# One written order for the opening of a local-attention and mixture block

## The chip, the cores and the metric

The kernel runs on 1 core of one Trainium2 chip. The metric is the device time of one execution in microseconds. The engines are TensorE (PE, with its weight loads PEld), VectorE (DVE), ScalarE (ACT), GpSimd (POOL) and SyncE (SP), which issues the loads.

## What is computed

Attention over 4 batches, 8 heads, 576 positions and 64 columns, with a window of 128 and a bias that falls with distance; a gated layer on its result; then four small attention experts with a choice of two per position. The change is in the first two parts, whose reference is, cut:

```python
scores = np.where(mask, scale * (q @ kT) + bias, -1e9)       # mask: 0 <= i-j < 128
attn = softmax(scores);  x = attn @ v                        # -> [4, 576, 512]
h = np.maximum(x @ w_in, 0.0);  u, v = h[..., :512], h[..., 512:]
v_n = (v - mu) / np.sqrt(var + 1e-06)                        # over the last axis
v_s = np.einsum('ts,bsd->btd', w_spatial, v_n) + b_spatial[None, :, None]
gated = u * v_s                                              # then w_out and the experts
```

w_in (512 x 1024) comes as 64-bit floats. All matmuls that need precision are done as three passes over a high and a low part of each factor (PASSES, L36).

## The kernel before

**Decoding w_in.** Eight chunks of 128 x 512 numbers (512 KB each) are loaded (load_in, L191) and turned into a high and a low part. For chunk n, word_bits (L276) makes an absolute value on ACT (L281) and five operations on DVE (L284 to L289): max, shift, or, mask, multiply. add_in (L212) sums the two results on PE into a PSUM tile psw (two instructions with ident, one with one), and ACT copies the high part out. low_in (L225) makes the low part: for chunks 0 to 3 PE sums the same again into a second PSUM tile psl and subtracts the high part there (L231 to L233), and ACT copies it; for chunks 4 to 7 DVE subtracts (lo_part, L129). Chunks 0 to 3 hold the columns of v, 4 to 7 those of u.

**Attention.** Twenty tiles (b, j) of 128 positions, the fifth of a batch of 64. scores (L343) makes two halves g in PSUM (pool psS, two buffers); softmax (L361) runs per half on DVE a masked copy (L374, not for j = 0), four fused bias-and-minimum operations (L150), and at the end a sum, a reciprocal and a multiply (L380 to L382), with four exponentials on ACT between (L151). transposes (L385) turns the half on PE, ACT copies it (L393) and POOL cuts it in two by the window (L400, L401). attend (L404) multiplies with v, and take (L420) splits the result into x high (ACT) and x low (DVE, L129).

**Dense work of a batch.** v_tile (L431) five times with statistics, normalised (L457), u_half twice (L493, 96 matmuls together), spatial (L507, 112 matmuls, gate multiply at L523). It sits in the list Dense (L39) and is pulled by a credit, RATE = 8200 ns of planned cost a step, when its tile is ready; a list entry that is not ready takes the credit to 0.

**Order.** PE's instructions run in the order of the program; all other engines are ordered by the planner's own costs. The program of the opening: some steps by hand for tiles 0 and 1 (L570 to L602), then the loop over s (L606): step s attends tile s-2, makes the scores of tile s, turns tile s-1, runs the softmax of tile s, and pulls dense work between; parts(s) (L561) puts in the chunks 4 to 7 and, at s = 6 to 8, the spatial weights (setup, L247). A barrier without waits for the planner stands at the top of each step. At s = 9 the buffers of the opening are closed. Where s = 8 starts, 22 of the 112 spatial matmuls of batch 0 are done.

Of the kernel before, what the change touches and what calls it, by code (L numbers as in the profile page):

```python
# [9 lines left out]
F32 = mybir.dt.float32  # L10
# [3 lines left out]
U32 = mybir.dt.uint32  # L14
# [21 lines left out]
PASSES = ((0, 0), (0, 1), (1, 0))  # L36

# [65 lines left out]
def block_kernel(ctx, tc, qP, kP, v, w_in, wspT, bsp, w_outT, wcat, wo, rel, relt, low, tri, out):  # L103
# [97 lines left out]
    def bits(n):  # L201

        if not is64:
            return
        f = early.tile([P, 512], F32, tag="f", name=f"f{n}", bufs=2)
        w = u[n % 4][:, :512]
        live[n] += [w, f]

        for _ in word_bits(w, f, live[n][0], in_parts(n)[1]):
            pass  # L210

    def add_in(n):  # L212

        hi, lo = in_parts(n)
        if is64:
            w = live[n][1]
            ps = psD.tile([P, 512], F32, tag="D", name=f"psw{n}")
            nc.tensor.matmul(ps, ident, w, start=True, stop=False)
            nc.tensor.matmul(ps, one, lo, start=False, stop=True)
            live[n].append(ps)  # L220
            nc.scalar.copy(hi, ps)
        else:
            nc.scalar.copy(hi, live[n][0])

    def low_in(n):  # L225
        hi, lo = in_parts(n)
        if is64:
            w, ps = live[n][1], live[n][3]
            if n < 4:
                ps = psD.tile([P, 512], F32, tag="D", name=f"psl{n}")  # L230
                nc.tensor.matmul(ps, ident, w, start=True, stop=False)  # L231
                nc.tensor.matmul(ps, one, lo, start=False, stop=False)
                nc.tensor.matmul(ps, minus, hi, start=False, stop=True)  # L233
                nc.scalar.copy(lo, ps)
            else:
                lo_part(lo, ps, hi)
        else:
            lo_part(lo, live[n][0], hi)
        decoded[0] = n + 1
# [7 lines left out]
    def setup():  # L247
        def spatial_weights(k):
            s0, sn = TOK[k]
            st = d2.tile([P, S], F32, tag="f64w", name=f"st_wsp{k}", bufs=2)  # L250
            for r in range(0, P, sn):
                nc.sync.dma_start(st[r : r + sn, :], wspT[s0 : s0 + sn, :])
            yield
            nc.scalar.copy(wsp[0][:, k, :], st)
            yield
            lo_part(wsp[1][:sn, k, :], st[:sn, :], wsp[0][:sn, k, :])
            yield

# [65 lines left out]
    def load_chunk(b, j):  # L324

        q0, qn = TOK[j]
        Q_[b, j] = a1.tile([P, 4, P], F32, tag="q", name=f"q{b}_{j}", bufs=3)
        nc.sync.dma_start(Q_[b, j], qP[b, :, j])
        if j == 0:
            K_[b] = a1.tile([P, 4, S], F32, tag="k", name=f"k{b}")  # L330
        if b == 0:
            nc.sync.dma_start(K_[b][:, :, q0 : q0 + qn], kP[b, :, :, q0 : q0 + qn])
        elif j == 0:
            nc.sync.dma_start(K_[b], kP[b])
        V_[b, j] = a1.tile([P, 512], F32, tag="v", name=f"v{b}_{j}", bufs=5)
# [7 lines left out]
    def scores(b, j):  # L343
# [17 lines left out]
    def softmax(b, j, g):  # L361

        ps = st_[b, j, g]
        p = a1.tile([P, 4, P], F32, tag="p", name=f"p{b}_{j}_{g}", bufs=3)
        st = a1.tile([P, 8], F32, tag="stat", name=f"st{b}_{j}_{g}", bufs=4)
        if j == 4:
            nc.vector.copy_predicated(ps[:, :, 0:64], lowm[:, 128:192].unsqueeze(1).to_broadcast([P, 2, 64]), ps[:, :, 128:192])
            for h in range(2):
                row_softmax(p[:, h, :], ps[:, h, 0:P], reltail[:, 2 * g + h, :], st[:, h : h + 1], st[:, 4 + h : 5 + h])
            n = 2  # L370
        else:
            view = ps.rearrange("p o (h c) -> p (o h) c", h=2)
# [691 lines left out]
```

## Time and profile before

| | us |
|---|---|
| median of 3 runs (506.79 to 507.25) | 506.8 |
| the profiled execution | 506.48 |
| its span, first to last instruction | 504.7 |
| PE busy, weight loads busy | 483.2, 423.5 |
| DVE, ACT, POOL busy | 308.5, 260.7, 100.6 |
| mean granted PE clock | 0.993 of full |

Busy times are over the whole span. The opening, up to step s = 8 at 99.36 us, is a fifth of it. A matmul's busy time is modelled and overlaps the next one, so the cost of a matmul in a stream is the distance from one start to the next. A wait is named by what ended it. The kernel after ends its opening at the same step, s = 8.

### The profile page before, as it was taken

The page shows a single profiled execution, that of the slowest core. Times are in us where ns is not written, and L with a number is a line of the kernel's source. Part 1 is how long each engine was busy: PE and PEld are TensorE (multiplying, and loading weights), DVE is VectorE, ACT ScalarE, POOL GpSimd, SP SyncE. Part 2 cuts the span into 40 slices and gives each one's busy share as a digit, 9 for nine tenths or more (in the row PEclk, how much of TensorE's full clock was granted, in tenths as well). Part 3 has the DMA queues.
Part 4 walks back from the last instruction along what each step waited for, and adds up shares of the span by engine and source line. Part 5 has one row for each costly group of instructions (what it writes and reads, how often), then busy time and mean ns, then how long its engine had stood idle before and what let it go on. Part 6 is the DMA issues. An engine that isn't in the chain of part 4 may idle for free.

```text
span 504.7 us, 10536 instructions
## 1 busy us (share of the span) xinstructions
PE 483.2 (96%) x3910; PEld 423.5 (84%) x3910; DVE 308.5 (61%) x1069; ACT 260.7 (52%) x778; POOL 100.6 (20%) x209
## 2 busy tenths in 40 slices
PE   8979879999999999999999999999999999999995
PEld 6547668898988989899888999998888899897873
DVE  4978887565888767875464624365484565555431
ACT  4665467533666436563344414256564555546562
POOL 1012211222102212112121010112322233232131
PEclk9998989999999999999999999999999999999999
DMA  8941233315231451201305650330000000002231
GB/s 282 373 141 43 63 90 103 116 69 191 87 95 44 183 192 43 95 2 48 111 1 155 206 196 1 95 95 1 1 23 2 2 23 1 1 1 85 84 105 64
DMA packets 25063, 44.34 MB, mean 88 GB/s; under 512 B 5810, under 2 KB 8242, under 8 KB 24628
## 3 DMA queue, kind: packets, MB, share of 16 engines
q1 hardware_dynamic: 24868, 43.54, 26.0%
q8 instruction: 31, 0.51, 0.4%
q14 instruction: 20, 0.16, 0.1%
q10 hardware_dynamic: 144, 0.13, 0.1%
HBM read 32.13 MB, written 11.53 MB: 87 GB/s over the span
## 4 chain that ended last, share of the span: by engine, by line
PE 75%; DVE 7%; ACT 6%; issue 6%; DMA 2%; POOL 2%; SPq 0%; POOLq 0%; ACTq 0%
PE pg L517 10%; PE pq L781 10%; PE pv L437 7%; PE pvB L805 6%; PE pu L500 5%; PE pxB L907 5%; PE pout L928 5%; PE ptB L889 4%; PE psB L846 4%; PE px L416 4%; PE pw L680 3%; PE ps L355 3%; PE pt L392 2%; ACT p L151 2%; PE pg L522 2%
## 5 line engine op out<-in xcount | busy, mean ns | idle before, releaser
L151 ACT ACTIVATE p<-p,st 128x128 f32<-128x128 f32 x144 | 56.2, 392 | 38.7 <-DVE st L150 38.7
L437 PE MATMUL pv<-win,x 128*128 128x512 f32 x240 | 63.6, 408 | 0.7 <-ACT x L132 0.7
L781 PE MATMUL pq<-x,W 128*128 128x288 f32 x384 | 58.3, 302 | 0.8 <-DVE k L129 0.8
L517 PE MATMUL pg<-wsp,vn 128*128 128x288 f32 x384 | 58.9, 298 | 0.1
L400 POOL TENSOR_SCALAR_AFFINE_SELECT pU<-pT 128x512 f32<-128x512 f32 (+1 forms) x32 | 23.2, 725 | 166.4 <-ACT pT L393 166.4
L500 PE MATMUL pu<-x,win 128*128 128x288 f32 x384 | 55.3, 298 | 0.0
L781 PEld LDWEIGHTS pq<-x,W 128*128 128x128 f32 x384 | 51.9, 188 | 3.6 <-DVE k L129 1.5
L158 POOL TENSOR_SCALAR pB<-pB,stB 128x128 f32<-128x128 f32 (+4 forms) x72 | 39.0, 560 | 78.8 <-DVE stB L869 62.5
L517 PEld LDWEIGHTS pg<-wsp,vn 128*128 128x128 f32 x384 | 52.9, 188 | 1.3 <-issue 1.0
L500 PEld LDWEIGHTS pu<-x,win 128*128 128x128 f32 x384 | 52.0, 188 | 2.0 <-issue 0.8
L437 PEld LDWEIGHTS pv<-win,x 128*128 128x128 f32 x240 | 44.0, 192 | 9.9 <-ACT x L132 0.8
L151 ACT ACTIVATE pB<-pB,stB 128x128 f32<-128x128 f32 (+3 forms) x64 | 35.7, 559 | 21.4 <-DVE stB L150 21.4
L150 DVE CUSTOM_DVE_ANT_0 pB<-psB,trit 128x128 f32<-128x128 f32 (+3 forms) x64 | 28.2, 486 | 10.0 <-PE psB L846 9.2
L805 PE MATMUL pvB<-W,x 128*128 128x260 f32 (+1 forms) x240 | 34.2, 289 | 0.0
L928 PE MATMUL pout<-wo,o 128*128 128x512 f32 x108 | 30.8, 412 | 0.9 <-ACT o L132 0.9
L805 PEld LDWEIGHTS pvB<-W,x 128*128 128x128 f32 (+1 forms) x240 | 29.9, 178 | 1.7 <-issue 1.7
L889 PE MATMUL ptB<-ident,pB 128*128 128x128 f32 (+1 forms) x200 | 30.7, 273 | 0.0
L392 PE MATMUL pt<-ident,p 128*128 128x128 f32 x144 | 23.0, 278 | 8.0 <-DVE x L129 6.3
L355 PE MATMUL ps<-k,q 64*128 64x256 f32 (+1 forms) x256 | 29.6, 373 | 0.6 <-DMA k<-in_kP 0.6
L150 DVE CUSTOM_DVE_ANT_0 p<-ps,relm 128x128 f32<-128x128 f32 x128 | 29.5, 286 | 0.8 <-PE ps L355 0.3
L907 PE MATMUL pxB<-pTB,vt 128*64 128x128 f32 (+2 forms) x480 | 28.3, 262 | 1.4 <-ACT pTB L890 1.4
L416 PE MATMUL px<-pT,v 128*64 128x128 f32 (+1 forms) x320 | 28.5, 272 | 0.3 <-POOL pT L401 0.3
(148 smaller groups left out, 879.8 us busy)
## 6 DMA issues: line engine op xcount, KB each, us to landing
q<-in_qP SPq DMA_DIRECT2D x20, 256.0 KB, 3.3
g_dram<-g SPq DMA_DIRECT2D x16, 288.0 KB, 2.1
raw<-in_w_in SPq DMA_DIRECT2D x8, 512.0 KB, 6.8
v<-in_v SPq DMA_DIRECT2D x16, 256.0 KB, 3.0
gf<-g_dram SPq DMA_DIRECT2D x4, 1024.0 KB, 5.3
out<-ot SPq DMA_DIRECT2D x15, 256.0 KB, 2.0
k<-in_kP SPq DMA_DIRECT2D x3, 1152.0 KB, 5.9
rawo<-in_w_outT SPq DMA_DIRECT2D x4, 512.0 KB, 4.2
```

The costliest lines, as they stand in the source:

```text
L150: nc.vector.tensor_tensor_reduce(s_view, ps_view, tab, -0.125, FLT_MAX, ALU.add, ALU.min, nm)
L151: nc.scalar.activation(s_view, s_view, AF.Exp, bias=nm, scale=-1.0, accum_out=sm)
L355: nc.tensor.matmul(ps[:, o, 256 * h : 256 * h + kn], Q_[b, j][r, hp, :], K_[b][r, hp, k0 : k0 + kn], start=True, stop=True)
L416: nc.tensor.matmul(px[64 * o : 64 * o + 64, hp, :qn], V_[b, t][:, h * 64 : h * 64 + 64], rhs, start=(t == max(0, j - 1)), stop=(t == j))
L437: nc.tensor.matmul(pv, x[i][:, k, t0 : t0 + P], win[j][:, k, 512:1024], start=(n == 0), stop=(n == 11))
L500: nc.tensor.matmul(pu[:, :HALF], win[i][:, k, m * P : (m + 1) * P], x[j][:, k, c], start=(n == 0), stop=(n == 11))
L517: nc.tensor.matmul(pg[:, :HALF], vn[i][k][:, m * P : (m + 1) * P], wsp[j][:, k, c], start=(n == 0), stop=False)
L781: nc.tensor.matmul(pq[:, :HALF], W[i][:, k, c0 : c0 + P], G[j][:, k, c], start=(n == 0), stop=(n == 11))
L805: nc.tensor.matmul(pv[:tn, :260], G[i][:, k, COL[t] : COL[t] + tn], W[j][:, k, 512:772], start=(n == 0), stop=(n == 11))
L889: nc.tensor.transpose(pt[:kb, n, :], p[pr][:, o, c0 : c0 + kb], ident)
L907: nc.tensor.matmul(px[64 * o : 64 * o + 64, pr, :qn], vt[:kb, c, (2 * pr + o) * 64 : (2 * pr + o) * 64 + 64], rhs, start=(c == 0), stop=(c ...
L928: nc.tensor.matmul(po[:tn], o2[i][:, pr, :tn], wos[j][:, pr, :], start=(n == 0), stop=(n == 5))
```

## The change

The steps 0 to 7 of the loop, the hand-written start, the decoding of all eight chunks, the spatial weights and batch 0's dense work are cut into single named operations. A string OPENING lists 486 of them, and step(name) issues them one by one; within this block ACT, DVE, POOL and SP too run in the order of the program, not the planner's. The names: rawN, kN, qN, vN, relN, low, reltail are loads; C3.shl an operation of chunk 3; s2.0 the scores of tile 2, half 0; l2.0.1 a logit operation (l2.0.cp the masked copy), e2.0.1 an exponential, f2.0.add, rec, mul the end of the softmax; t, c, g the turn, its copy and its cuts; a2 attention, xh2 and xl2 the split; V2.0 a third of v tile 2, r, bn, ag its statistics; n and N the normalisation; U0.2.1 a third of u half 0, block 2; ur its copy; W2.ld, hi, lo the spatial weights; P and pm the spatial matmuls and gate multiplies. "+11" puts eleven transposes of the identity ahead of the operation (fill).

The tiles run in the order 0, 2, 3, 1, 4, 6, 5, 7. All chunks are treated alike: the high part is subtracted in the PSUM tile of the sum (minus), and ACT copies the low part; the second sum of chunks 0 to 3 and DVE's subtraction of chunks 4 to 7 are gone. The starting transposes go from 22 + 10 + 10 to 28, and 40 are put in as fill. Buffers of vr go from 3 to 5. The loop begins at s = 8; what is left of batch 0 (SECOND, THIRD: 16 u matmuls, two low parts of vn, all 112 spatial matmuls) stands first in the dense list. For the other batches the list is as before.

```diff
+OPENING = """
+    k3 rel0 raw0 k0 q0 k4 k2 C0.abs low C0.max raw1 C0.shl s0.0+11 C0.or s0.1 raw2 l0.0.0 C0.sum C0.mask e0.0.0 l0.0.1 C0.mul e0.0.1 raw3 l0.0.2 C0.add
+    l0.0.3 e0.0.2 l0.1.0 l0.1.1 C1.abs l0.1.2 l0.1.3 raw4 e0.0.3 C1.max e0.1.1 f0.0.add C1.shl e0.1.2 f0.0.rec C1.or e0.1.3 q1 C0.high f0.0.mul C1.sum+20
+    e0.1.0 q2 C1.mask C2.abs f0.1.add t0.0 rel1 C1.mul C0.minus c0.0 C2.max k1 C1.add f0.1.rec C2.shl C3.abs raw5 f0.1.mul C1.high C2.or C0.low t0.1+5
+    C1.minus C3.max q3 c0.1 C2.sum C2.mask C1.low C3.shl reltail C2.mul s2.0 v0 C3.or C4.abs raw6 C2.add l2.0.cp s2.1 C2.high C4.max l2.0.0 C2.minus v1
+    l2.0.1 C3.sum e2.0.0 l2.1.cp e2.0.1 v2 l2.0.2 a0 C2.low l2.1.0 l2.0.3 v3 e2.1.0 l2.1.1 l2.1.2 e2.0.3 l2.1.3 s3.0 v4 C3.mask e2.1.1 C4.shl e2.1.2 k5
+    C3.mul s3.1 e2.0.2 xh0 l3.0.cp C5.abs C3.add f2.0.add xl0 C3.high l3.0.0 e2.1.3 f2.0.rec l3.0.1 C3.minus f2.0.mul e3.0.0 C3.low raw7 f2.1.add C4.or
+    t2.0+4 e3.0.1 V0.0 f2.1.rec l3.0.2 c2.0 l3.1.cp e3.0.2 W0.ld g2.0.0 V0.1 f2.1.mul W1.ld g2.0.1 l3.1.0 l3.1.1 t2.1 e3.1.0 l3.1.2 l3.1.3 V0.2 e3.1.1
+    C4.mask c2.1 l3.0.3 C4.mul e3.0.3 s1.1 g2.1.0 r0 C5.max f3.0.add C5.shl C6.abs g2.1.1 C4.sum f3.0.rec l1.1.cp W0.hi a2 f3.0.mul W1.hi l1.1.0 e3.1.2
+    C5.or e1.1.0 W1.lo e3.1.3 C5.sum xh2 f3.1.add l1.1.1 f3.1.rec l1.1.2 e1.1.1 l1.1.3 C4.add xl2 e1.1.2 s1.0 C4.high f3.1.mul e1.1.3 t3.0 bn0 q4 V2.0
+    c3.0 l1.0.cp q5 g3.0.0 t3.1 f1.1.add ag0 l1.0.0 q6 f1.1.rec C4.minus l1.0.1 e1.0.0 g3.0.1 V2.1 f1.1.mul c3.1 l1.0.2 e1.0.1 l1.0.3 g3.1.0 t1.1 C5.mask
+    e1.0.2 C6.max s4.0 C4.low g3.1.1 C5.mul c1.1 s4.1 l4.0.cp C7.abs C6.shl g1.1.0 a3 l4.0.0 e1.0.3 q7 l4.1.cp g1.1.1 e4.0.0 l4.0.1 f1.0.add l4.1.0 e4.0.1
+    f1.0.rec C6.or e4.1.0 f1.0.mul C5.add xh3 C6.sum f4.0.add l4.1.1 C5.high f4.0.rec xl3 s6.1 e4.1.1 f4.0.mul C6.mask t1.0 C7.max C5.minus C6.mul c1.0
+    V2.2 l6.1.cp C5.low g1.0.0 t4.0 C7.shl r2 C6.add l6.1.0 g1.0.1 s5.1 l6.1.1 c4.0 l6.1.2 V3.0 e6.1.0 bn2 g4.0.0 e6.1.2 l5.1.0 g4.0.1 e6.1.1 l6.1.3 a1
+    l5.1.1 e5.1.0 ag2 l5.1.2 e6.1.3 f4.1.add l5.1.3 f4.1.rec C6.high C7.or e5.1.1 f4.1.mul e5.1.2 C6.minus C7.mask v5 V3.1 xh1 W0.lo C6.low v6 xl1 V3.2
+    e5.1.3 W2.ld C7.mul t4.1 f5.1.add r3 V1.0 W3.ld f6.1.add f5.1.rec f6.1.rec f5.1.mul c4.1 v7 g4.1.0 V1.1 f6.1.mul g4.1.1 bn3 V1.2 W2.hi ag3 t5.1 W2.lo
+    W3.hi C7.sum c5.1 W3.lo W4.ld r1 C7.add t6.1 W5.ld C7.high bn1 s5.0 c6.1 C7.minus ag1 l5.0.0 q8 s6.0 n2.ln g6.1.0 l5.0.1 C7.low l5.0.2 l5.0.3 e5.0.2
+    g6.1.1 a4 l6.0.cp e5.0.1 W4.hi l6.0.0 U0.2.0 l6.0.1 e5.0.3 v8 l6.0.2 W4.lo e6.0.1 U0.1.0 e6.0.2 U0.0.0 l6.0.3 e6.0.0 e6.0.3 s7.0 xh4 f6.0.add f6.0.rec
+    e5.0.0 U0.0.1 f6.0.mul n2.ex W5.hi U0.0.2 f5.0.add l7.0.cp s7.1 f5.0.rec xl4 ur0.0 l7.0.0 U0.2.1 f5.0.mul e7.0.0 t6.0 l7.0.1 U0.2.2 l7.0.2 e7.0.1
+    l7.0.3 W5.lo U0.1.1 c6.0 e7.0.3 U0.1.2 n2.r0 g6.0.0 n2.r1 ur0.2 n2.r2 t5.0 e7.0.2 n2.r3 g6.0.1 N2.sc V4.0 ur0.1 l7.1.cp c5.0 N2.hi N0.sc V4.1 l7.1.0
+    N0.hi N2.lo U1.3.0 e7.1.0 l7.1.1 l7.1.2 U1.2.0 e7.1.1 l7.1.3 N0.lo e7.1.2 U1.3.1 e7.1.3 N1.sc V4.2 f7.0.add f7.1.add N1.hi f7.0.rec f7.1.rec f7.0.mul
+    U1.2.1 r4 f7.1.mul U1.2.2 U0.3.0 bn4 ur1.2 U0.3.1 N1.lo U0.3.2 ag4 n4.ln U1.3.2 n4.ex ur0.3 n4.r0 a5 n4.r1 ur1.3 n4.r2 n4.r3 N3.sc U1.1.0 N4.sc xh5
+    U1.0.0 N3.hi xl5 q9 v9
+"""
+FIRST = """
+
+"""
+SECOND = """
+    U1.0.1 N4.hi N3.lo U1.0.2 N4.lo U1.1.1 ur1.0 U1.1.2 P0.0.0 ur1.1
+"""
+THIRD = """
+    P0.0.1 P0.0.2 P0.1.0 pm0.0 P0.1.1 P0.1.2 P1.0.0 pm0.1 P1.0.1 P1.0.2 P1.1.0 pm1.0 P1.1.1 P1.1.2 P2.0.0 pm1.1 P2.0.1 P2.0.2 P2.1.0 pm2.0 P2.1.1 P2.1.2
+    P3.0.0 pm2.1 P3.0.1 P3.0.2 P3.1.0 pm3.0 P3.1.1 P3.1.2 pm3.1
+"""
...
+        elif name == "sum":
+            live[n].append(psD.tile([P, 512], F32, tag="D", name=f"psw{n}"))
+            fill(live[n][3][:, :P])
+            nc.tensor.matmul(live[n][3], ident, live[n][1], start=True, stop=False)
+        elif name == "add":
+            nc.tensor.matmul(live[n][3], one, lo, start=False, stop=True)
+        elif name == "high":
+            nc.scalar.copy(hi, live[n][3])
+        elif name == "minus":
+            nc.tensor.matmul(live[n][3], minus, hi, start=False, stop=True, skip_group_check=True)
         else:
...
+            nc.scalar.copy(lo, live[n][3])
+
+    idle = [0]
+
+    def fill(ps):
+        for _ in range(idle[0]):
+            nc.tensor.transpose(ps, ident, ident)
+        idle[0] = 0
...
+    E_ = mybir.EngineType
+    with tc.manual_schedule(engines={E_.Activation, E_.DVE, E_.Pool, E_.SP}):
+        warm(28)
+        for name in OPENING.split():
+            step(name)
+    decoded[0] = 9
+    for name, names in (("u0_0", FIRST), ("u0_1", SECOND), ("s0", THIRD)):
+        dense.add(rest(names), cost(names), name=name)
+    for b in range(1, B):
...
-    for s in range(2, len(tiles) + 2):
+    for s in range(8, len(tiles) + 2):
```

## Rows read from the trace of the kernel before

**Rows 1.** Busy time by stretch: time, engines' busy (instructions), PEclk, DMA share.
```profile
core 0: us, PE busy (x) PEld busy (x) DVE busy (x) ACT busy (x) POOL busy (x), PEclk, DMA share, GB/s
0.00:29.32 29.32, 26.51 (x143) 18.49 (x143) 18.99 (x69) 17.60 (x52) 1.47 (x11) 1.00 0.86 293
29.32:99.36 70.04, 61.15 (x453) 49.54 (x451) 57.45 (x197) 43.07 (x141) 14.56 (x23) 0.95 0.30 95
99.36:260.00 160.64, 159.37 (x1324) 143.88 (x1325) 110.19 (x392) 80.26 (x267) 30.77 (x44) 1.00 0.27 91
```

**Rows 2.** Timeline, PE: start, us, engine, line, operation; first v tile, step s=8.
```profile
29.32 2.11 PE L437 MATMUL pv<-win,x 128*128 128x512 f32 x8
...
99.36 0.44 PE L416 MATMUL px<-pU,v 128*64 128x128 f32 x4
...
101.25 2.00 PE L355 MATMUL ps<-k,q 64*128 64x256 f32 x16
```

**Rows 3.** Timeline, PE: stretches in which it ran on.
```profile
27.07 0.39 PE L233 MATMUL psl<-win,minus 128*128 128x512 f32 x1
27.39 2.00 PE L355 MATMUL ps<-k,q 64*128 64x256 f32 x16
...
54.46 2.09 PE L437 MATMUL pv<-win,x 128*128 128x512 f32 x8
56.39 1.02 PE L218 MATMUL psw<-u,ident 128*128 128x512 f32 x2
...
57.48 0.60 PE L392 MATMUL pt<-ident,p 128*128 128x128 f32 x4
57.84 1.17 PE L437 MATMUL pv<-win,x 128*128 128x512 f32 x4
...
79.72 5.12 PE L500 MATMUL pu<-x,win 128*128 128x288 f32 x36
84.78 1.09 PE L416 MATMUL px<-pT,v 128*64 128x128 f32 x16
```

**Rows 4.** Groups by line, DVE, 0 to 99.36: count, busy us, mean ns, idle.
```profile
L150 DVE CUSTOM_DVE_ANT_0 p<-ps,relm 128x128 f32<-128x128 f32 x56 | 13.0, 285 | 0.6 <-PE ps L355 0.3
L382 DVE TENSOR_TENSOR p<-p,st 128x512 f32<-128x512 f32 x14 | 9.8, 699 | 0.3
L374 DVE COPY_PREDICATED ps<-lowt,ps 128x512 f32<-128x512 uint16 x10 | 6.9, 690 | 0.1
...
L129 DVE TENSOR_TENSOR win<-psw,win 128x512 fp32r<-128x512 f32 x4 | 2.7, 671 | 0.1
...
L381 DVE RECIPROCAL st<-st 128x4 f32<-128x4 f32 x14 | 2.5, 176 | 0.3
L473 DVE TENSOR_SCALAR vr<-vr,vs 128x512 f32<-128x512 f32 x5 | 2.5, 543 | 0.1
```

**Rows 5.** Timeline, 0 to 45 us: ACT's first chunk operation, DVE's first operation.
```profile
5.25 0.67 ACT L281 ACTIVATE f<-raw 128x512 f32<-128x512 f32 x1 [2.65 <-DMA raw<-in_w_in]
...
5.95 0.43 DVE L284 TENSOR_SCALAR f<-f 128x512 f32<-128x512 f32 x1 [5.95 <-ACT f L281]
```

**Rows 6.** DMA view, 0 to 40 us: rate in each microsecond.
```profile
GB/s 0 37 197 254 259 362 401 313 324 418 410 377 340 347 412 385 359 333 365 329 387 389 397 410 383 324 55 29 0 0 70 368 406 406 194 8 0 0 0 0
```

**Rows 7.** DVE's waits, 0 to 99.36: us in total, times, longest us.
```profile
DVE f L284 <- ACT f L281: 9.1, 3, 5.9
DVE st L380 <- ACT p L151: 5.1, 9, 1.1
...
DVE x L129 <- ACT x L132: 0.6, 2, 0.4
```

**Rows 8.** Busy time in steps of 2 us, columns as in rows 1.
```profile
36.00:38.00 2.00, 0.04 (x2) 0.07 (x3) 2.00 (x7) 2.00 (x9) 0.12 (x1) 1.00 0.00 0
38.00:40.00 2.00, 2.00 (x22) 2.00 (x24) 1.93 (x6) 0.42 (x1) 1.16 (x2) 0.55 0.00 0
40.00:42.00 2.00, 2.00 (x18) 1.64 (x17) 1.86 (x5) 0.49 (x1) 0.00 (x0) 0.60 0.03 8
```

More of the change, by code (lines that the diff above doesn't have):

```diff
@@ L199, in in_parts, with chunk @@
         return [win[i][:, k, half * 512 : half * 512 + 512] for i in range(2)]
-    def bits(n):
+    def chunk(n, name):
+        hi, lo = in_parts(n)
         if not is64:
[L204 to L221, printed above, removed]
-        else:
-            nc.scalar.copy(hi, live[n][0])
@@ L225, in low_in @@
[L225 to L239, printed above, removed]
+            if name == "high":
+                nc.scalar.copy(hi, live[n][0])
+            elif name == "low":
+                lo_part(lo, live[n][0], hi)
+        elif name == "abs":
+            f = early.tile([P, 512], F32, tag="f", name=f"f{n}", bufs=2)
+            w = u[n % 4][:, :512]
+            live[n] += [w, word_ops(w, f, live[n][0], lo)]
+            live[n][2]["abs"]()
+        elif name in ("max", "shl", "or", "mask", "mul"):
+            live[n][2][name]()
+        elif name == "sum":
[8 more added lines that the diff above has]
+            nc.tensor.matmul(live[n][3], minus, hi, start=False, stop=True, skip_group_check=True)
+        else:
+            nc.scalar.copy(lo, live[n][3])
@@ L390, in transposes, with turn @@
         before = None
-        for i in range(n):
-            nc.tensor.transpose(pt[:, i, :], p[:, i, :], ident)
-        nc.scalar.copy(here[:, :n], pt[:, :n])
+        def turn():
+            fill(pt[:, 0, :])
+            for i in range(n):
+                nc.tensor.transpose(pt[:, i, :], p[:, i, :], ident)
+        ops = {"t": turn, "c": lambda: nc.scalar.copy(here[:, :n], pt[:, :n])}
         if j > 0:
@@ L407, in attend @@
         px = psT.tile([P, 4, P], F32, tag="T", name=f"px{b}_{j}")
+        fill(px[:, 0, :])
         for hp in range(4):
@@ new lines, in normal_ops, with normalised, u_ops, part @@
+        return ops
+    def normalised(st, tiles):
+        ops = normal_ops(st, tiles)
+        yield lambda: (ops["ln"](), ops["ex"]())
+        yield lambda: [ops[f"r{i}"]() for i in range(4)]
+        for t in tiles:
+            for name in ("sc", "hi", "lo"):
+                yield ops[f"{name}{t}"]
+    def u_ops(b, s, m):
+        c = slice(s * HALF, (s + 1) * HALF)
+        pu = psD.tile([P, 512], F32, tag="D", name=f"pu{b}_{m}_{s}")
+        fill(pu[:, :P])
+        def part(n):
+            i, j = PASSES[n]
+            for k in range(4):
+                nc.tensor.matmul(pu[:, :HALF], win[i][:, k, m * P : (m + 1) * P], x[j][:, k, c], start=(n == 0 and k == 0), stop=(n == 2 and k == 3))
+        ops = {f"U.{n}": lambda n=n: part(n) for n in range(3)}
+        ops["ur"] = lambda: nc.scalar.activation(u[m][:, c], pu[:, :HALF], AF.Relu)
+        return ops
```

422 lines of the change are left out of this document (234 added, 188 removed).

## The prediction

> **What bounds the kernel now.** I read the table by stretches first [rows 1]. From 99.36 us on, TensorE (PE) is busy in 159.37 of 160.64 us, so there the matmuls set the time, and microseconds won ahead of that point are won at the end. Ahead of it PE is not the limit: its weight loads fill 18.49 of the first 29.32 us and 49.54 of the next 70.04, against 143.88 of 160.64 later. VectorE (DVE) fills 57.45 of those 70.04. So the opening is the stretch from 0 to 99.36, cut in two where the first v tile starts and closed where step s=8 starts with its attention matmuls [rows 2]. The change writes steps 0 to 7 anew and leaves the loop from s=8 as it is: the question is when PE reaches that point, and with how much dense work done.
>
> The Trainium skill (Perfetto Trace Analysis, Identifying the Most-Contended Engine) says that matmul busy time misleads and that weight-load time should be used. By PE's busy column only 8.9 us of the 70.04 would be idle, and no order could win more there; by the prices below it is 14.4. The weight-load column of the same row sides with the second reading.
>
> **PE's work between the first v tile and s=8, at clean prices.** These are distances between starts in stretches where PE ran on [rows 3]: eight v matmuls in 56.39 - 54.46 = 1.93, so 2.9 for a v tile of 12; 36 u matmuls in 84.78 - 79.72 = 5.06, so 0.141 each, also taken for the spatial ones; 16 score matmuls in 29.32 - 27.39 = 1.93; a turn of four transposes 57.84 - 57.48 = 0.36; a chunk's sum and add 57.48 - 56.39 = 1.09; the minus matmul 0.39. Attention of a full tile is 101.25 - 99.36 = 1.89 [rows 2], of a batch's first tile 1.09 [rows 3]. Estimates from these: scores of a tail tile 1.3, of a first tile 1.1; attention of a tail tile 1.2; a tail's two turns 0.3.
> Before, 29.32 to 99.36: five v tiles 14.5, 96 u matmuls 13.5, 22 spatial ones 3.1, scores of five tiles 3 x 1.93 + 1.3 + 1.1 = 8.2, attention of five 3 x 1.89 + 1.2 + 1.09 = 8.0, turns 10 x 0.36 + 0.3 = 3.9, four chunks 4.4. Sum 55.6, so 14.4 of 70.04 us go into waits and a slow clock.
> After, from V0.0 to the end of OPENING: v 14.5, 80 u matmuls 11.2, scores of tiles 1, 4, 5, 6, 7 8.2, attention of tiles 1 to 5 8.0, turns 9 x 0.36 + 0.3 = 3.5, four chunks with the added minus 5.9. Sum 51.3. What before had done at 99.36 and after has not (the 16 u matmuls in SECOND and 22 spatial ones) is 38 x 0.141 = 5.3, all of it on PE's path and charged to the change.
>
> **DVE's work.** It was busy 18.99 + 57.45 = 76.4 us before s=8 [rows 1]. The change takes off four low parts of the late chunks (4 x 0.67), moves two low parts of vn (the same subtraction, 2 x 0.67) and one gate multiply (288 of 512 columns, estimated at 0.4) behind the opening [rows 4]: 72.0 are left. In the list the last operation that PE's scores must wait for is l6.0.3, which frees the score buffer of s7.1. Behind it DVE has four softmax ends 4 x (0.70 + 2 x 0.18) = 4.2, two logit halves 2 x (0.69 + 4 x 0.23) = 3.2, five scalings 2.5, five subtractions 5 x 0.67 = 3.3, eight small refinements and the last statistics 2.2, estimated from the 0.18 row: 15.4 [rows 4]. So 56.6 us of DVE work stand ahead of l6.0.3.
>
> **Where DVE starts.** Now raw0 is the first load, its absolute value runs at 5.25 and DVE starts at 5.95 [rows 5]. In the list k3 and the first bias table stand ahead of raw0, 512 KB; at the 259 to 362 GB/s of microseconds 4 and 5 [rows 6] that is 1.4 to 2 us: DVE starts at 7.6. Everything in DVE's order waits for that. The loads behind it keep ahead: k1, the last that s2.0 needs, ends about 5.2 MB, which the rates of rows 6 reach at 17 us, and DVE comes to s2.0 at about 19. raw4 must wait on SP's queue for C0.mul, with q1, q2, rel1 and k1 behind it; C0.mul is done at about 10.5, when some 0.8 MB are still queued ahead, so it costs nothing; 2 us later this cover would be gone.
>
> **The head up to V0.0: no change.** Ahead of V0.0 the list gives DVE chunks 0 to 3, tile 0, tile 2 and parts of chunk 4 and tile 3, about 20.5 us at these prices, against 18.99 before plus 29.32 - 5.95 - 18.99 = 4.4 of waits. 7.6 + 20.5 + 1 for waits gives V0.0 at 29.1; I keep 29.3. Chunks 0 to 3 lose a second sum and add on PE (4 x 1.09) and one PSUM buffer each, but PE waits here. The 40 filling transposes (at 0.36 / 4 each, 3.6 us) stand in PE's waits too: nothing, or 3.6 if DVE is early. The four late low parts become ScalarE (ACT) copies; ACT is busy 43.07 of 70.04 us [rows 1]: nothing. Turning the generator code into named steps issues the same instructions.
>
> **Sum with no wait at all.** By PE: 29.3 + 51.3 = 80.6. By DVE: 7.6 + 56.6 = 64.2, and then PE has scores of tile 7, 17 thirds of u tiles, a v tile, two turns and an attention, 1.93 + 9.6 + 2.9 + 0.72 + 1.09 = 16.2: 80.4. The two bounds meet, so the list is balanced and slack in neither. With the 5.3 still owed, parity with 99.36 comes at 85.9: at most **13.5 us** to win.
>
> **What the waits take back.** Every engine now runs one fixed order, so an operation that is not ready holds all behind it. In the list I counted the places ahead of l6.0.3 where DVE's next operation needs another engine's result and less DVE work than that result takes stands between: seventeen (scores to logits for s0.0, s2.0, s2.1, s4.0, s5.0, s6.0; last exponential to row sum for e0.0.3, e0.1.0, e1.0.3, e3.0.3, e3.1.3; C1.abs, C4.abs; W2.hi, W3.hi, W4.hi; r1). No row shows them; rows 7 bound them: 0.3 each where DVE waits for a split's copy (0.6 in 2), 0.57 where it waits for the exponentials (5.1 in 9), and nothing where PE or ACT runs ahead of the list. I take 0.3, since most are one short operation late, as the split is: 17 x 0.3 = 5.1. The 9.1 us that DVE waits for the chunks' absolute values, three waits of up to 5.9 [rows 7], I take as gone, because chunks 4 to 7 are loaded and converted as buffers come free; what is late next is ACT and PE handing over to DVE, which these seventeen price.
>
> **Behind s=8.** The dense list trails by 2.7 us of the planner's cost after s=9 and catches up where before runs out of ready tiles (before loses 2.7 of credit at s=20, by the list's costs and the 8.2 per step), so the order of the last steps is the same. PE is full there [rows 1], and I carry the gain to the end.
>
> **Forecast.** 13.5 - 5.1 = 8.4 us off the profiled 506.48: 498.1; the median is 0.3 higher: **498.4**.
>
> **Rivals.**
> (a) Dear handovers: each costs 0.57 as with the exponentials: 9.7, gain 3.8, 503.0. For it: the list often puts a row sum right behind its last exponential. Against: half of the seventeen aren't of that kind.
> (b) The list runs as written, waits near nothing: 493.3 to 495. For it: its own sums balance to 0.2 us. Against: seventeen tight places.
> (c) Slower, by lock-step: a stalled engine stalls those that feed it, and the cost of one handover grows. From 13.5 / 17 = 0.8 us a place the change loses; at the longest split-free wait of rows 7, 1.1, it is 18.7, so 5.2 slower: 512. The Trainium skill (TensorE: Matmul & The Clock Gate, on queue depths) has ACT's and DVE's queues as strict first-in first-out, eight deep; by that rule nothing behind a late operation can fill in, which is this rival. Against it in the trace: DVE's queue was in a fixed order before too, and its waits for exponentials and splits came to 5.7 us in the whole opening.
> (d) The clock: PE's granted clock was 0.55 and 0.60 of full speed, near its lower level, over 38 to 42 us, after 2 us in which it was busy for 0.04 [rows 8]. One such fall loses 2 x 0.45 + 2 x 0.40 = 1.7 us; it takes five beside the seventeen handovers to eat the forecast gain. Against: the new order leaves no wait so long behind V0.0.
> (e) That it doesn't shift the end: the loop behind 99.36 would have to be limited by something other than PE, which rows 1 don't show.
>
> **Chances.** Forecast, 495 to 500.5: 0.53. (b) 0.12. (a) with part of (d), 500.5 to 505.8: 0.20. Within 0.2% of before, which is about what a measurement of this kernel can tell from no change: 0.05. (c) and (d) full: 0.10. So faster 0.85, same 0.05, slower 0.10. The range goes from 493 (no waits) to 504 (past rival a), which leaves out the slower cases, the same ones and a little of (a).
>
> **What would show each step.** DVE's first operation near 7.6; V0.0 near 29; PE's turn to s=8 near 85.7 with 16 u matmuls still to come; DVE busy near 72 up to there; DVE's waits on exponentials and scores about 5 us in total, and none on raw chunks behind the first; the granted clock at full behind V0.0. I am wrong if raw0 or k1 lands 2 us later than worked out, if the handovers cost 0.8 each, or if PE after s=8 shows waits that before has not.

## The result, and the profile after

The changed kernel takes 500.27 us (median of 4, 497.77 to 500.81) where the kernel before takes 506.8: ratio 0.986, 95% interval 0.983 to 0.989. In a second set of runs it took 498.99, ratio 0.986 (0.984 to 0.988). The prediction was 498.4, in a range of 493 to 504. The profiled execution took 499.99 us, its span 498.3; that of before 506.48, its span 504.7. Two executions, one of 539.28 us (DVE's order alone) and one of 1599.21 (no fills), stand far from the others of their kernels and are left out of the medians below.

Three rows of the changed kernel say where the opening stands now. Two are from the timeline of TensorE (PE): start, us, engine, line, operation, and in brackets the idle time before it with its releaser. The scores line is the one that answers to the last row of [rows 2].

```profile
30.02 2.09 PE L511 MATMUL pv<-win,x 128*128 128x512 f32 x8
...
84.56 0.44 PE L473 MATMUL px<-pU,v 128*64 128x128 f32 x4 [0.25 <-DVE x L164]
...
86.45 2.00 PE L397 MATMUL ps<-k,q 64*128 64x256 f32 x16
```

The scores of step s=8 start at 86.45 instead of 101.25, 14.8 us earlier. 5.3 us of PE work is still owed there, so the opening won **9.5 us**. Yet the end moved by 6.4. The table by stretches (columns as in [rows 1]) shows PE with less slack and the granted clock at full:

```profile
0.00:30.02 30.02, 24.84 (x160) 18.50 (x161) 19.47 (x74) 18.19 (x55) 1.47 (x11) 1.00 0.90 294
30.02:84.56 54.54, 53.75 (x416) 41.96 (x414) 50.98 (x187) 44.46 (x141) 15.44 (x22) 1.00 0.36 118
84.56:250.00 165.44, 164.16 (x1356) 148.15 (x1356) 113.56 (x395) 80.91 (x269) 30.10 (x45) 1.00 0.27 89
```

From the first v tile to s=8 PE took 54.54 us for work of 51.3 at clean prices; before it was 70.04 for 55.6. So 11.2 of the 14.4 us that waits and clock took there are gone. The kernel before's matmul column showed only 8.9 us idle in that stretch [rows 1]; the change took more than that out of it. That decides the weighing made in the prediction, as far as the clean prices hold. The Trainium skill (Perfetto Trace Analysis, Identifying the Most-Contended Engine) has matmul busy time as a poor measure of what is left and names the share of the weight loads, with the share of peak arithmetic, in its place; the 11.2 against 8.9 agree with that.

VectorE's (DVE's) waits up to s=8 (us in total, times, longest), against [rows 7]:

```profile
DVE f L315 <- ACT f L314: 9.0, 1, 9.0
DVE ps L415 <- PE ps L397: 1.7, 3, 0.7
DVE st L422 <- ACT p L187: 0.7, 1, 0.7
DVE vs L534 <- ACT vs L533: 0.6, 1, 0.6
DVE vs L523 <- ACT vr L520: 0.6, 1, 0.6
DVE wsp L164 <- ACT wsp L288: 0.5, 1, 0.5
DVE p L186 <- PE ps L397: 0.2, 1, 0.2
```

The first is the start, of which more below. The six rows behind it, eight waits, come to 4.3 us, and the waits for exponentials fell from 5.1 us in nine to 0.7 in one.

**What was given back.** The gain is still nearly whole late in the loop: the attention of tile 18 starts at 246.30 instead of 258.42, with 20 u matmuls (2.8 us) still owed, which leaves 9.3 us. At the fold, the first work behind the loop, nothing is owed any more and 6.8 are left. One place lies between. There the timeline shows ScalarE (ACT), DVE and PE over the split of tile 18's attention output, px, which PE had finished at about 248.3:

```profile
248.84 1.46 DVE L541 TENSOR_SCALAR vr<-vr,vs 128x512 f32<-128x512 f32 x3
249.42 1.14 ACT L544 CAST vn<-vr 128x512 fp32r<-128x512 f32 x2 [1.42 <-DVE vr L541]
250.22 1.28 DVE L164 TENSOR_TENSOR vn<-vr,vn 128x512 fp32r<-128x512 f32 x2
250.47 0.58 ACT L485 CAST x<-px 128x512 fp32r<-128x512 f32 x1
...
251.42 0.68 DVE L164 TENSOR_TENSOR x<-px,x 128x512 fp32r<-128x512 f32 x1
...
252.16 0.69 PE L442 MATMUL pt<-ident,p 128*128 128x128 f32 x2 [2.12 <-DVE x L164]
```

The planner has put the normalisation of batch 3's first tiles (scaling vr, casts and low parts vn) ahead of the two halves of the split. ACT's cast of px, ready to run at 248.3, starts at 250.47, DVE's low part at 251.42, and PE's next turn, which needs the PSUM buffer that px holds, waits 2.12 us. Before, the same turn waits 0.89:

```profile
263.04 0.44 PE L392 MATMUL pt<-ident,p 128*128 128x128 f32 x2 [0.89 <-DVE x L129]
```

The table in steps of 2 us shows what follows:

```profile
250.00:252.00 2.00, 0.04 (x1) 0.00 (x0) 2.00 (x4) 1.88 (x5) 0.00 (x0) 1.00 0.00 0
252.00:254.00 2.00, 1.84 (x8) 1.84 (x9) 0.70 (x2) 0.37 (x1) 0.56 (x2) 0.50 0.00 0
254.00:256.00 2.00, 2.00 (x12) 2.00 (x11) 0.00 (x0) 0.41 (x1) 0.28 (x1) 0.65 0.00 0
256.00:258.00 2.00, 2.00 (x18) 2.00 (x17) 0.00 (x0) 0.67 (x2) 0.46 (x2) 1.00 0.00 0
```

PE's granted clock falls to 0.50 and 0.65: 2 x 0.50 + 2 x 0.35 = 1.7 us lost. Together 1.2 + 1.7 = 2.9, where 9.5 - 6.8 = 2.7 are missing at the fold. The last 0.4 of the 3.1 us between 9.5 and 6.4 go behind the fold: PE's one wait for W there is 1.2 us, where the kernel before waits 0.8 for k. The kernel before has its falls of the clock in the opening instead [rows 8].

### The profile page after: what moved, and what is told of

It reads as the page before. It is cut to its first block, busy times and chain, and to the rows that moved or that the text cites. A ratio compares the mean times of both kernels' runs of the same rounds, so it can differ in the third digit from the quotient of the medians.

```text
span 498.3 us, 10577 instructions
## 1 busy us (share of the span) xinstructions
PE 480.9 (97%) x3928; PEld 422.5 (85%) x3928; DVE 305.6 (61%) x1065; ACT 264.2 (53%) x782; POOL 100.8 (20%) x209
## 4 chain that ended last, share of the span: by engine, by line
PE 83%; DVE 9%; ACT 3%; DMA 3%; issue 1%; SPq 1%; ACTq 0%
PE pq L901 11%; PE pg L602 10%; PE pv L511 10%; PE pu L575 8%; PE pvB L925 6%; PE pxB L1027 5%; PE pout L1048 5%; PE px L473 4%; PE ptB L1009 4%; PE psB L966 4%; PE ps L397 4%; PE pw L800 3%; PE pt L442 3%; PE pg L605 2%; PE psB L968 1%; DMA q<-in_qP 1%
## 5 line engine op out<-in xcount | busy, mean ns | idle before, releaser
L511 PE MATMUL pv<-win,x 128*128 128x512 f32 x240 | 61.5, 400 | 0.7 <-ACT x L485 0.7
L575 PE MATMUL pu<-x,win 128*128 128x288 f32 x384 | 58.0, 303 | 0.0
L575 PEld LDWEIGHTS pu<-x,win 128*128 128x128 f32 x384 | 53.7, 192 | 3.1 <-issue 2.3
L451 POOL TENSOR_SCALAR_AFFINE_SELECT pU<-pT 128x512 f32<-128x512 f32 (+1 forms) x32 | 21.7, 679 | 151.2 <-ACT pT L444 151.1
L444 ACT COPY pT<-pt 128x512 f32<-128x512 f32 (+1 forms) x40 | 21.5, 537 | 14.7 <-PE pt L442 14.6
L397 PEld LDWEIGHTS ps<-k,q 64*128 64x128 f32 x256 | 21.3, 186 | 9.2 <-issue 5.1
```

What stands on the lines that cost most here:

```text
L397: nc.tensor.matmul(ps[:, o, 256 * h : 256 * h + kn], Q_[b, j][r, hp, :], K_[b][r, hp, k0 : k0 + kn], start=True, stop=True)
L511: nc.tensor.matmul(pv, x[i][:, k, t0 : t0 + P], win[j][:, k, 512:1024], start=(n == 0 and k == 0), stop=(n == 2 and k == 3))
L575: nc.tensor.matmul(pu[:, :HALF], win[i][:, k, m * P : (m + 1) * P], x[j][:, k, c], start=(n == 0 and k == 0), stop=(n == 2 and k == 3))
```

## The experiments

Every set had the kernel before beside it (medians 506.2 to 506.7). The changed kernel itself was run again in one set only, with "raw0 first", "split first" and "catch-up"; the later sets are held against that run. One table shows where each kernel stood in its profiled execution. In the first row and the last two, which are built on the kernel before, 5.3 us more work is done at s=8 than in the others, so of the kernel before 95.95 is to be compared.

| kernel | first v tile | scores of s=8 | fold's first matmul (pw) | span | median us |
|---|---|---|---|---|---|
| before | 29.32 | 101.25 | 293.94 | 504.7 | 506.8 |
| changed | 30.02 | 86.45 | 287.12 | 498.3 | 500.27 |
| changed, again | 30.52 | 86.95 | 287.65 | 498.8 | 498.99 |
| raw0 first | 28.64 | 85.08 | 285.82 | 496.9 | 497.25 |
| split first | 30.75 | 87.25 | 284.12 | 495.2 | 496.85 |
| both | 27.77 | 84.22 | 281.07 | 492.2 | 494.31 |
| both, all splits | 27.41 | 83.91 | 280.20 | 491.3 | 493.10 |
| catch-up | 30.3 | 86.77 | 288.80 | 499.9 | 501.17 |
| planner's order | 34.02 | 98.57 | 305.61 | 516.7 | 519.28 |
| DVE's order alone | 31.39 | 97.63 | 299.15 | 510.2 | 511.95 |
| ACT's order alone | 33.08 | 92.14 | 291.33 | 502.4 | 504.40 |
| no fills | 31.17 | 87.75 | 296.34 | 507.4 | 506.27 |
| before, merged decoding | 28.26 | 101.76 | 294.45 | 505.6 | 506.90 |
| before, split first | 29.26 | 102.08 | 294.56 | 506.0 | 505.42 |

**The changed kernel again**, as the measure for the runs of its set.

> The changed kernel once more, beside the others of this group. Theory: it ends near 500.3 us with one long wait of TensorE of about 2 us at the last attention tile (near 250 us) and a granted clock near one half for some 4 us behind it; an execution in which the clock does not fall there ends near 497.8. Rival: the 3 us that are missing behind the opening are spread over many steps, and no single wait of more than 1 us shows.

498.99 us (498.68 to 500.49). The wait of 2.12 us at the split of tile 18 is there again at 252.60. The fall of the clock behind it does not seem to be in every execution: the one profiled (500.49) has a mean clock of 0.997, the other three, at 498.7 to 499.0, a full one. A fall of 1.7 us would make 0.997 of a full clock over 498.8 us, and the times differ by 1.5; the other three were not traced.

**The dense list without its lag.** The list of dense work starts the loop 2.7 us of planner's cost behind; this kernel takes that away.

```diff
     outw = iter(())
+    dense.credit = 2690.0
```

> Edit: the credit of the dense list starts at 2690 ns at s = 8, which is what the list trails behind that of the kernel before. Theory (the trailing list puts the normalisation of the last batch's first three tiles onto the split of tile 18, and the split is late): the last steps get the order they had before, the wait near 250 us falls from 2.1 to about 0.9 and the clock stays at full: 497.5, and the executions agree within 1 us. Rival (the loss comes from something else behind s = 8): 500 as the changed kernel.

It took 501.17 (499.8 to 501.66), not the 497.5 that I expected. The last steps are as before the change, with a wait of 0.90 at the same turn and a full clock. But the same collision has moved to batch 2, at 190.60, and three smaller ones, the 0.90 among them, stand beside it. The timeline row of the large one, and then PE's waits of that kind in the whole run:

```profile
190.60 0.41 PE L442 MATMUL pt<-ident,p 128*128 128x128 f32 x2 [2.08 <-DVE x L164]
```

```profile
PE pt L442 <- DVE x L164: 4.0, 4, 2.1
```

So the lag chooses the place, but taking it away doesn't take the loss away. In both places where a normalisation fell on a split, the planner ordered the split behind the start of it; in these two kernels the shift of the dense list only chose the batch in which that happened.

**The split first.** The direct cut: from s=20 on, the planner may put nothing from behind the split ahead of it. The barrier is one of the planner's alone; it adds no instruction and leaves PE's order as it was.

```diff
             take(*tiles[s - 2], px)
+            if s >= 20:
+                tc.no_sync_barrier()
```

> Edit: from s = 20 on the planner may move nothing from behind the split of the attention (take) ahead of it; VectorE and ScalarE do the split of tile 18 ahead of the normalisation. The list goes on trailing. Theory: the wait of 2.1 us goes, the clock stays at full, 497.0 to 497.5. Rival (the trailing list costs by itself, through less ready work): the wait stays above 1 us and the time near 500.

496.85 us (496.51 to 497.69), ratio 0.981 (0.980 to 0.983), close to the 497.0 to 497.5 that I expected. The turn now runs straight behind the u matmuls, as PE's timeline shows, and the clock is full from 244 to 264:

```profile
248.96 1.84 PE L575 MATMUL pu<-x,win 128*128 128x288 f32 x12
250.64 0.38 PE L442 MATMUL pt<-ident,p 128*128 128x128 f32 x2
```

From s=8 to the fold this kernel needs 196.87 us, the changed one 200.70 beside it: 3.8 less, the wait of 2.1 and the fall of 1.7.

**The same barrier in the kernel before**, as a control.

> The kernel before with the barrier alone (from s=20 on, behind the split of the attention output). It is the control for the barrier's 2.1 to 3.6 us in the changed kernel. Theory (the changed kernel gives back some 3 us because its normalisation now falls on the split of tile 18): in the kernel before that wait is 0.9 us and the clock stays full, so the barrier brings at most 1 us: 505.6 to 506.6. Rival (the barrier is a gain of its own, unrelated to what the change lost): 503 to 504.5.

505.42 us, ratio 0.998 (0.997 to 0.999). PE's waits of this kind behind s=8 went from the first of these rows to the second:

```profile
PE pt L392 <- DVE x L129: 1.5, 3, 0.9
...
PE pt L392 <- DVE x L129: 0.2, 1, 0.2
```

The medians differ by 1.3, which is that. (The second row is from the longest execution of its kernel, 507.76 us with a mean granted clock of 0.939, so its times in the table are not compared.) So of what the barrier brings the changed kernel, 1.3 us were to be had before too. The rest is 0.8 by the medians (2.1 - 1.3) and 2.5 in the traced executions (3.8 - 1.3), in which the clock falls: a longer wait and the clock that it costs came with the change.

**raw0 first.** The first chunk of w_in, the first keys and queries are issued ahead of the bias tables; k3 and k4 go behind k1. The order on PE, DVE and ACT is the same as in the changed kernel.

```diff
-    k3 rel0 raw0 k0 q0 k4 k2 C0.abs
+    raw0 k0 q0 rel0 k2 C0.abs
...
-    C2.max k1 C1.add
+    C2.max k1 k3 k4 C1.add
```

> Edit: order of the first loads alone. raw0, k0, q0, rel0, k2 come first; k3 and k4 go behind k1. In the changed kernel raw0 was third and VectorE started at 9.0 us instead of 5.95. Theory (VectorE's order bounds the opening from its first instruction on): VectorE starts at about 6, the first v tile at 27.5 instead of 30.0, step s = 8 at 82 instead of 84.6, and the time falls by 2 to 2.5 us to about 498. Rival (the next load, raw1 or k1, or the score inputs become the wait): VectorE starts at 6 but waits about as much a little later; s = 8 stays within 0.5 us of 84.6 and the time within 0.5 us of the changed kernel's.

497.25 us (496.78 to 498.64), 1.7 below the changed kernel beside it. DVE starts at 5.83, as in the timeline's row below, instead of 9.02 and 9.58; the scores of s=8 come 1.9 earlier, and so does the end.

```profile
5.83 0.43 DVE L315 TENSOR_SCALAR f<-f 128x512 f32<-128x512 f32 x1 [5.83 <-ACT f L314]
```

Of 3.7 us won at the start, half arrives, less than the 2 to 2.5 that I expected: in exchange DVE waits 1.9 us more for scores in other places (3.7 against 1.8), at one of them behind a wait of PE of 1.2 for keys.

What made raw0 late as the third load is shown by SyncE's row for it and by three microseconds of the changed kernel (columns as in [rows 1]):

```profile
2.19 0.43 SPq L235 DMA_DIRECT2D raw<-in_w_in  x1
...
4.00:5.00 1.00, 1.00 (x7) 1.00 (x6) 0.00 (x0) 0.00 (x0) 0.00 (x0) 1.00 0.84 197
5.00:6.00 1.00, 1.00 (x7) 1.00 (x6) 0.00 (x0) 0.00 (x0) 0.00 (x0) 1.00 0.39 140
6.00:7.00 1.00, 1.00 (x10) 1.00 (x9) 0.00 (x0) 0.00 (x0) 0.00 (x0) 1.00 0.62 210
```

In the kernel before raw0 is issued at 0.79 and first used at 5.25, here at 2.19 and 8.33. So 1.4 of the 3.1 us are the later issue, and 1.7 a longer time from issue to use. In microseconds 4 to 6 the DMA engines moved only 140 to 210 GB/s, although they did not lack issued loads: by 3.90 SyncE had issued 1.5 MB, of which some 0.45 MB had been moved by 4.00. What held them is not shown.

**Both edits.**

> Both edits that won alone: the first raw chunk, k0 and q0 issued ahead of k3, the bias tables behind them (alone 497.25, 1.7 below the changed kernel run beside it), and the barrier from s=20 on that keeps the split of the tile ahead of the normalisation (alone 496.85, 2.1 below). Theory: the two sit at different ends of the run, the one moves PE's arrival at s=8, the other takes a wait of 2.1 us and a clock fall out of the last steps, so they add up: 494.7 to 495.7, first DVE operation near 5.9, scores of s=8 near 85.1, no wait over 1 us on the split of the last batch's tiles. Rival: both gains are one and the same thing, the chance position of the dense work against the last steps: then about 496.8 to 497.3, no better than either alone.

494.31 us (493.88 to 495.87), ratio 0.977 (0.975 to 0.978). The two gains add up: 1.7 + 2.1 would give 495.2, and it is 0.9 below that.

**The barrier at every split from s=8 on.**

```diff
-            if s >= 20:
+            if s >= 8:
```

> The fastest version so far (first raw chunk ahead, barrier from s=20 on; 494.3) with the barrier behind every split from s=8 on. Theory: the planner puts other work ahead of a split only where the normalisation coincides with it, which the trace shows once in this kernel, at s=20: PE's other waits behind s=8 come to 0.9 us on pT copies, so nothing more is to be had: 493.8 to 494.8. Rival 1: the barriers bind VectorE and ScalarE where they were free to run ahead, and their results come late: 496 to 500. Rival 2: the small waits go too: 493.0 to 493.5.

493.10 us (492.75 to 494.02), ratio 0.973 (0.971 to 0.974), **the fastest version**, 5.9 us below the second median of the changed kernel. I expected no more gain; the small waits did go too (copies of pT held PE for 0.9 us, now 0.5, and a split for 0.4, now nothing), but a new one of 0.6 for POOL's part of vn has come. The table shows 0.3 of the 0.9 us of span at s=8 already, with the same code up to there; the rest comes between s=8 and the fold. These waits make 0.2 of it; what the rest is, I can't say.

**The planner's order.** The same list and the same order on PE, but DVE, ACT, GpSimd and SyncE are ordered by the planner.

```diff
-    with tc.manual_schedule(engines={E_.Activation, E_.DVE, E_.Pool, E_.SP}):
-        warm(28)
-        for name in OPENING.split():
-            step(name)
+    warm(28)
+    for name in OPENING.split():
+        step(name)
```

> The same list of operations with the same TensorE order, but VectorE, ScalarE, GpSimd and SyncE are ordered by the planner, as in the kernel before, instead of by the list. Theory A (the gain of the opening comes from one written order on all engines): the planner puts VectorE operations that PE does not need next ahead of those it does, and PE's written order waits for them: arrival at s=8 several us after the 84.6 to 87 of the changed kernel, time 502 to 508. Theory B (the gain comes from PE's new order and the merged decoding alone): arrival at s=8 within 1 us of the changed kernel, time 498 to 500.5.

519.28 us (517.92 to 521.82): theory A in kind, and larger. The scores of s=8 start at 98.57, 11.6 after the changed kernel run again and 2.6 after before's 95.95. PE's new order and the merged decoding lose without the written order on the other engines; **with this list, that order is worth more than the whole gain of the opening**. (The order of the tiles and the five buffers of vr are in all of these runs; they were not tried alone.) PE's waits up to s=8 show it, and a stretch of DVE's timeline shows how:

```profile
PE pt L442 <- DVE p L424: 3.6, 2, 2.2
...
PE pt L442 <- DVE x L164: 2.7, 1, 2.7
```

```profile
43.14 0.75 DVE L164 TENSOR_TENSOR wsp<-st_wsp,wsp 128x576 fp32r<-128x576 f32 x1
43.81 0.68 DVE L319 SCALAR_TENSOR_TENSOR win<-raw,f 128x512 fp32r<-128x512 uint32 x1
...
46.26 0.68 DVE L164 TENSOR_TENSOR x<-px,x 128x512 fp32r<-128x512 f32 x1
```

The low part of the spatial weights, which no one needs for long, and w_in's decoding stand ahead of the split that PE's next turn waits for. Another 6.3 us are lost between s=8 and the fold (207.04 against 200.70), where the planner's order has changed as well.

**DVE's written order alone, and ACT's alone.**

```diff
-    with tc.manual_schedule(engines={E_.Activation, E_.DVE, E_.Pool, E_.SP}):
+    with tc.manual_schedule(engines={E_.DVE, E_.SP}):
```

> As the changed kernel, but in the opening the written order holds for VectorE, SyncE and PE alone; ScalarE and GpSimd are ordered by the planner. With no written order at all but PE's, step s=8 came 11.6 us later. Theory (VectorE's order carries the gain, since VectorE is the engine whose work and start bound the opening): s=8 within 2 us of the changed kernel, time 499 to 501. Rival (ScalarE's order carries it): s=8 8 to 12 us later, time 508 to 515.

511.95 us, with s=8 at 97.63, 10.7 late: my theory fell. The counterpart has E_.Activation in place of E_.DVE.

> The counterpart: the written order holds for ScalarE, SyncE and PE; VectorE and GpSimd are ordered by the planner. Theory (VectorE's order carries the gain): s=8 8 to 12 us later than in the changed kernel, time 508 to 515. Rival (ScalarE's order carries it): s=8 within 2 us, time 499 to 501. If both this and its counterpart stay near 499, one written order is enough to hold the other engine to it, by the results that they wait for.

504.40 us, s=8 at 92.14, 5.2 late, between what the theory and the rival give. With no written order s=8 is 11.6 late; DVE's takes 0.9 off that, ACT's 6.4, each together with SyncE's, and the changed kernel, where GpSimd's is written as well, all of it. What SyncE's and GpSimd's orders bring by themselves was not tried. The timeline of the kernel with DVE's order alone shows what one misplaced instruction does, on ACT, PE and DVE:

```profile
36.15 0.67 ACT L288 CAST wsp<-st_wsp 128x576 fp32r<-128x576 f32 x1 [4.56 <-DMA st_wsp<-in_wspT]
36.73 0.58 ACT L444 COPY pT<-pt 128x512 f32<-128x512 f32 x1
...
37.36 1.12 PE L442 MATMUL pt<-ident,p 128*128 128x128 f32 x4 [3.90 <-ACT pT L444]
...
39.84 0.17 DVE L422 TENSOR_SCALAR st<-st 128x4 f32<-128x4 f32 x1 [5.72 <-ACT p L187]
```

The planner set the cast of the spatial weights ahead of the copy of pT, and its load wasn't there. ACT stood for 4.56 us with work that was ready behind the cast; PE stood 3.90 for the copy, DVE 5.72 for the exponentials behind it. Over 36 to 44 us PE's clock is 0.55, 0.50, 0.50 and 0.74. In the changed kernel's list the same cast stands behind the first v rows, and ACT waits for nothing there. This is the lock-step of rival (c), with its price. By the Trainium skill (TensorE: Matmul & The Clock Gate, on engine queue depths) ACT's and DVE's queues are strict first-in first-out; the trace agrees, as in this stretch nothing overtook the cast in 4.56 us.

**No fills.** The 40 filling transposes of the list are left out (every `+11`, `+20`, `+5`, `+4`).

> The 40 filling transposes of the list are taken out, nothing else; they compute nothing that is used. Theory: they stand in waits of PE ahead of the first v tile and cost nothing, as worked out in the prediction: first v tile and arrival at s=8 within 0.5 us, time 498.5 to 499.5. Rival 1: they are on PE's path: up to 3.6 us faster, 495.5. Rival 2: without them the granted clock falls in the waits ahead of the first v tile: each fall as in the kernel before 1.7 us, time 500 to 503.

506.27 us (nine executions from 504.6 to 509.2), ratio 1.000 (0.998 to 1.003): the whole gain is gone. By the clock this is rival 2, by the time more than it gave, and the clock ahead of the first v tile is only a little of it. The trace is of the longest of the nine, 509.18. In steps of 4 us from 8 us on:

```profile
8.00:12.00 4.00, 1.50 (x14) 1.53 (x16) 1.78 (x6) 0.66 (x1) 0.00 (x0) 0.74 1.12 351
12.00:16.00 4.00, 3.01 (x9) 1.12 (x7) 3.95 (x23) 3.54 (x16) 0.00 (x0) 0.50 0.88 294
16.00:20.00 4.00, 3.79 (x9) 2.12 (x10) 3.81 (x10) 2.29 (x7) 0.00 (x0) 0.50 0.96 321
20.00:24.00 4.00, 3.74 (x20) 2.06 (x21) 2.97 (x7) 3.12 (x7) 0.00 (x0) 0.98 0.96 307
```

PE runs at half its clock for 8 us, and it costs 0.65 us at the first v tile and 0.8 at s=8, since PE waits for others there. The other 8 us arise behind s=8: 208.59 us to the fold against 200.70. There PE's order is the same, but the planner's orders on DVE and ACT have come out otherwise from about 134 us on, and new waits stand in PE's list:

```profile
PE pg L602 <- ACT vn L544: 1.3, 1, 1.3
PE pu L575 <- ACT u L578: 1.2, 1, 1.2
PE pg L602 <- ACT u L578: 1.1, 1, 1.1
PE pg L605 <- POOL vn L552: 1.1, 1, 1.1
```

with a further fall of the clock, to 0.50 over 280 to 284 us. So this run doesn't measure the fills alone: taking them out changed the planner's later orders, and that is most of the price in this execution. What the fills are worth with those orders held was not tried.

**The merged decoding alone**, on the kernel before: every chunk's low part by a minus matmul into the sum's buffer and a copy on ACT.

```diff
-            w, ps = live[n][1], live[n][3]
-            if n < 4:
...
-            else:
-                lo_part(lo, ps, hi)
+            ps = live[n][3]
+            nc.tensor.matmul(ps, minus, hi, start=False, stop=True, skip_group_check=True)
+            nc.scalar.copy(lo, ps)
```

> One part of the change alone, on the kernel before: every chunk of w_in has its low part taken by one matmul with the negative identity into the sum's own PSUM buffer and a ScalarE copy (before: chunks 0 to 3 by a second sum into another buffer, chunks 4 to 7 by a VectorE subtraction). Theory: VectorE loses 4 x 0.67 = 2.7 us of work before s=8, but what ends the opening there is the order and its waits, so little of it arrives: 505.5 to 506.8. Rival 1: VectorE's work is the bound of the opening: 2.7 less, 503.5 to 504.5. Rival 2: the low parts' copies queue on ScalarE behind exponentials: 507 to 508.

506.9 us, ratio 1.001 (1.000 to 1.002): no difference. DVE was busy for 74.72 us up to s=8 instead of 76.4, but the scores of s=8 came at 101.76, 0.5 later. PE now waits for ACT's copies of the high parts ahead of the minus matmuls, which the kernel before doesn't show among its longer waits:

```profile
PE psw L229 <- ACT win L221: 5.9, 4, 1.6
```

Three of the four lie ahead of the first v tile, which came at 28.26, 1.1 earlier, all the same; the fourth, 1.6 us at 35.95, lies behind it. So the merging brings nothing by itself. The run doesn't show that DVE's work is no bound, since it adds this wait; in the changed kernel other matmuls stand between the sum and the minus, and the same wait is 0.7.

## Why the prediction was right, and where it wasn't

- **PE's arrival at s=8**: worked out as 85.7, measured 84.56; the opening won 9.5 where 8.4 was forecast. By PE's path the sum was 29.3 + 51.3 + 5.1 and came out as 30.02 + 54.54: the start 0.7 later, what stands beside the clean prices 3.2 instead of 5.1. The argument that it is order and waits, not work, that the change removes is borne out: the merged decoding alone gave nothing, and with the list as it is the planner's order in place of the written one lost 11.6 us.
- **DVE's start**: 7.6 expected, 9.02 and 9.58 measured. The step that was mis-sized took the queue ahead of raw0 as 512 KB at the 259 to 362 GB/s of [rows 6], 1.4 to 2 us; it cost 3.1. SyncE's timeline shows k3 issued at 0.79 in 0.70 us, the bias table at 1.55 in 0.59, raw0 only at 2.19, which is 1.4; and the DMA engines then moved 197, 140 and 210 GB/s in microseconds 4 to 6, for a reason that is not shown, which is the other 1.7. With raw0 first the end is 1.7 us earlier.
- **The head**: V0.0 at 29.1 to 29.3 expected, 30.02 measured. The later start came through to 0.7 us: DVE was busy for 19.47 us up to there, where 20.5 were worked out, and waited 1.5 where 1 was.
- **DVE's work**: 72.0 expected, 19.47 + 50.98 = 70.45 measured.
- **The handovers**: 17 x 0.3 = 5.1 expected; DVE's eight waits behind the start are 4.3, of which one of 0.6, at 81.88, lies behind l6.0.3 and is none of the seventeen. The sum was near, its spread was not: seven waits of 0.2 to 0.7 us, and the other places show none.
- **PE behind the first v tile**: 51.3 at clean prices and 54.54 measured, so 3.2 more. PE's list of waits names 0.3 of it, and all its idle time there is 0.8; the rest lies in starts that follow each other later than at clean prices, the largest of them 0.6 behind a chunk's add. Whether it is the handovers that reach PE in this way, or the cost of changing from one short piece of work to the next, is not shown.
- **The fills**: they cost nothing, as worked out; without them s=8 came 0.8 later, not earlier. That leaving them out changes the planner's orders 100 us later was not seen.
- **Behind s=8**, the step that failed: "so the order of the last steps is the same", and with it "I carry the gain to the end". The order was not the same. The lag of the dense list moved batch 3's normalisation onto the split of tile 18; of the 3.1 us that were lost behind s=8, 2.7 went up to the fold, by a wait of 2.1 instead of 0.9 and the clock behind it, and 0.4 behind the fold, by a longer wait for W: rivals (d) and (e), in part, at a place where I saw neither. The barrier at the split took 3.8 back. Of that, the control in the kernel before shows, 1.3 were to be had there already.

That the forecast was near is in part luck, because two errors were opposed: 1.1 us too little for the opening, 3.1 too little for what was lost later. In executions in which the clock seems not to fall, at 498.7 to 499.0, the second is about half as large (3.1 - 1.5).

## What to carry to other kernels

When an engine's order is written by hand, write the orders of all engines that feed each other: one of the two compute engines' alone, with SyncE's, gave 0.9 or 6.4 of 11.6 us here. A stretch that a planner orders is not left as it was by an edit ahead of it; look in the new trace for the places where a slow chain (here a normalisation) falls on a result that PE waits for, and hold that result first. Put the load that starts the longest chain at the head of its queue, and count what is ahead of it in issues as well as in bytes: of 3.1 us of delay here, 1.4 were issues.

## What the runs showed of the hardware

- A load's issue held SyncE for 0.4 to 0.7 us in the first microseconds; raw0, issued from 2.19 to 2.62 as the third, was first used at 8.33, and as the first (from 0.79) at 5.14. With 1 MB issued and not yet moved, the DMA engines went down to a busy share of 0.39 and 140 GB/s for a microsecond.
- One wait of 2.1 us of PE, with nothing else to do, was followed by a granted clock of 0.50 and 0.65 over the next 4 us, and in the second traced execution of 0.81, 0.50 and 0.84 over 6. Three other executions of the same kernel show a mean clock of 1.000 instead of 0.997 and end 1.5 us earlier.
- A half clock of 8 us cost 0.8 us where PE was waiting for others anyway; behind s=8, where PE is the limit, taking out a wait of 2.1 with a fall of 1.7 brought 3.8.
